# Routed attention and a gated feed-forward block on one core: narrower key bands over cluster-sorted rows (112 places beyond a chunk instead of 128)

## The chip, the core and the metric

The kernel runs on one core of a Trainium2 chip. The core has TensorE (PE in the profile; its weight loads are PEld), VectorE (DVE), ScalarE (ACT), GpSimd (POOL) and SyncE (SP), each with its own queue that is worked off in order, 16 DMA engines, an on-chip memory (SBUF) of 128 partitions, and PSUM, into which TensorE writes. The metric is the device time of one execution in microseconds (us), as a median over runs.

## The reference

Attention for 4 batches of 8 heads, 768 positions, head width 64. Every query and every key belongs to the one of 16 centroids to which it is nearest by direction; a query attends only to keys of its own cluster. The result goes through a feed-forward block with hard-swish.

```python
q_assign = argmax(einsum('bhsd,hcd->bhsc', q_n, c_n));  k_assign = the same for k
mask   = q_assign[:, :, :, None] == k_assign[:, :, None, :]
scores = where(mask, q @ k.T / 8, -1e9)
attn   = softmax(scores);  x = (attn @ v), heads side by side      # (3072, 512)
h      = x @ w_in;  g = h * clip(h + 3, 0, 6) / 6;  out = g @ w_out  # d_ff 2048
```

## The kernel before

Heads are worked in 16 pairs (two heads of 64 make 128 partitions). The order of all instructions is written by hand: the kernel records them in one sequence, and every engine works off its own part of that sequence in order.

*Pairs 0 to 7 (batches 0 and 1)* use full attention: every chunk of 128 keys against all 768 queries, with a mask added through TensorE. During this stage the weights are decoded from 64-bit floats. It fills roughly the first third of the span.

*Pairs 8 to 15 (`FIRST` to `NPAIR - 1`)* sort first. `own_clusters`, `run_up`, `step_up`, `order` and `positions` work out, for every query and key, its place when the rows are sorted by cluster; `edges` keeps, per pair and cluster, the first place and the place behind the last, for queries (index 0) and keys (index 1). `scatter` (L1034) writes the rows of q, and of k and v together, to their places in DRAM: 24 indirect DMAs per pair from POOL, each followed by three tiny memsets (`pause`, L1026). `load_ranked` reads the sorted rows back over SP's queue (tiles `piece` for q and k, `vs` for v), and `turn_ranked` transposes them on TensorE (L919), with the copy out of PSUM on ACT (L920).

Then only a band of the score matrix is needed. `band(i)` says which chunks of queries the keys of chunk i meet: chunk i and its two neighbours, so 384 queries for the four inner chunks and 256 for the first and last. `band_scores` computes the bands in three steps: chunks 0, 5 and 1, then 2 and 3, then 4. Each band is, for each of the two heads, a bf16 mask product (`xm`, written by `band_masks` from the ends of the clusters) and an f32 product of keys and queries (L1077); chunks 1 and 3 use the two PSUM tiles `pv` and `pw`, the others `ps`. ACT takes the exponential (L1100) into tiles `be`, which come from a pool `bandp` of 5 buffers of 384 columns. `band_values` multiplies them with the values (L1116): each half of the queries (384) gets contributions of four chunks, the inner one first (all 384 columns), then parts of 256, 256 and 128 columns. `key_adds` adds, on DVE (L1130), the exponentials of the other three chunks onto those of the inner chunk (1 or 4); `band_sums` sums that over the keys on TensorE (L1140), and `band_divide` divides. `keep_ranked` writes the result in sorted order to DRAM, `gather` (L1050, 12 indirect DMAs per pair on POOL) brings it back to the original order, `turn_back` transposes it and stores it as input `xd` of the feed-forward block.

`steps_of` gives every step of a pair an offset in points; a pair has a slot of 28 points (`SLOT`), and `late_plan` lays the eight pairs over one another. For pair g the scatters are recorded at offset -24, `band_masks` at -12, `load_ranked` at -5, `turn_ranked` at -1 and 0, the bands at 2 to 12, the gather at 23 and `turn_back` at 37 (the last pair has some of them earlier). At 26 of the 28 points one item of the feed-forward block is recorded. `up` items (L659, 16 per block of 256 tokens) multiply with `w_in`, and their operand sums `tx` are fetched by DMAs that ACT issues two items ahead (L548); ACT then copies (`sx`, L677) and lifts (L499), DVE adds and clips (L670, L502, L649). `down` items (L698, 14 per block) multiply with `w_out`. The feed-forward block is computed by a scheme of seven half-size products in place of eight.

After the last pair only feed-forward items are left. There `whether_good` works out, on DVE, a flag from all range sums, among them a test on `edges`; when the flag is not set, `general_path` computes everything a second time without sorting.

Of the kernel before, what the change touches and what calls it, by code (L numbers as in the profile page):

```python
# [18 lines left out]
P = 128  # L19
# [19 lines left out]


FAR = 2.0**60


FIRST = NPAIR // 2
# [75 lines left out]
def fast_path(ctx, tc, ok, q, k, v, centroids, moe_w_in, moe_w_out, out):  # L120
# [660 lines left out]
    def whether_good():  # L781
        good = smallp.tile([P, 2, 2 * FIRST], F32, name="good")
        fit = smallp.tile([P, 2, NW], F32, name="fit")
        alone = smallp.tile([P, 2, FIRST], F32, name="alone")
        for got, sums, *bounds in (
            (good, totals, BOUND, 0.0), (fit, w_totals, W_HIGH, 0.0), (alone, counts, NC2, -NC2 * (C - 1.0)),
        ):
            for a, bound in enumerate(bounds):
                nc.vector.tensor_scalar(
                    out=got[:, a], in0=sums[:, a], scalar1=bound, scalar2=None, op0=ALU.is_le  # L790
                )
        low = smallp.tile([P, 6], F32, name="low")
        for a, got in enumerate((good, fit, alone)):
            nc.vector.tensor_reduce(out=low[:, a : a + 1], in_=got, axis=AX.XY, op=ALU.min)
        late = NPAIR - FIRST
        sane = smallp.tile([P, 2, late, 4 * NHC], F32, name="sane", tag="sane")
        flat = inverses.rearrange("p g i c -> p g (i c)")
        for a, (bound, op) in enumerate(((BOUND, ALU.is_le), (1.0 / BOUND, ALU.is_ge))):
            nc.vector.tensor_scalar(out=sane[:, a], in0=flat, scalar1=bound, scalar2=None, op0=op)
        nc.vector.tensor_reduce(out=low[:, 3:4], in_=sane, axis=AX.XYZ, op=ALU.min)  # L800
        near = smallp.tile([P, 2, late], F32, name="near")
        for a in range(2):
            nc.vector.tensor_tensor(
                out=near[:, a], in0=edges[:, :, a, 1], in1=edges[:, :, 1 - a, 0], op=ALU.subtract
            )
        nc.vector.tensor_scalar(out=near, in0=near, scalar1=P + 1.0, scalar2=None, op0=ALU.is_le)
        nc.vector.tensor_reduce(out=low[:, 4:5], in_=near, axis=AX.XY, op=ALU.min)
# [23 lines left out]
    def open_late():  # L831
        whole.close()
        late = ctx.enter_context(ExitStack())
        for name, bufs in (
            ("rankp", 1), ("piecep", 2), ("svp", 1), ("fromp", 1), ("natp", 1), ("sortp", 1), ("bandp", 5),
            ("rowp", 3), ("posp", 4),
        ):
            st[name] = right(late, name, bufs)
        for name, bufs in (("psum_y", 2), ("psum_s", 1)):
            st[name] = late.enter_context(tc.tile_pool(name=name, bufs=bufs, space=PSUM))  # L840
        rankp = st["rankp"]
# [90 lines left out]
    def own_clusters(g):  # L932
# [6 lines left out]
        mx = rankp.tile([P, 2 * NC2], F32, name="mx")  # L939
# [71 lines left out]

    def positions(g):
        prod = st.pop(("prod", g))
        posf = st["rankp"].tile([P, 2 * NC2], F32, name="posf")
        nc.vector.reduce_sum(out=posf, in_=prod, axis=AX.X)
        pos = st["pos", g] = st["posp"].tile([P, 2, NCH, 2], I32, name="pos")
        nc.vector.tensor_scalar(
            out=pos.rearrange("p a j t -> p (a j t)"), in0=posf, scalar1=S - 1.0, scalar2=0.0,
            op0=ALU.min, op1=ALU.max,
        )  # L1020
# [34 lines left out]

    def band_masks(g):
        xm = st["xm", g] = st["sortp"].tile([P, NC2, P], BF16, name="xmsort")
        ends = st["rankp"].tile([P, 2], F32, name="ends")
        nc.vector.tensor_scalar(
            out=ends, in0=edges[:, g - FIRST, :, 1], scalar1=st["sign"], scalar2=st["odd"],  # L1060
# [6 lines left out]
        nc.vector.tensor_scalar(out=xk, in0=st["places"], scalar1=ends[:, 1:2], scalar2=None, op0=ALU.is_lt)  # L1067

    def band(i):
        return max(i - 1, 0), min(i + 2, NCH)  # L1070

    def band_products(g, i, dst):
        lo, hi = band(i)
        for x, first in ((st["xm", g], True), (st["xs", g], False)):
            for t in range(2):
                r = slice(t * D, (t + 1) * D)
                nc.tensor.matmul(dst[t], lhsT=x[r, NCH + i], rhs=x[r, lo:hi], start=first, stop=not first)  # L1077

    def band_scores(g, pair, other=None):

        ps = st["psum_s"].tile([P, 2, 512], F32, name="ps")
        at, parts = 0, []
        for i in pair:
            w = (band(i)[1] - band(i)[0]) * P
            parts.append((i, w, [ps[:, :, at : at + w]]))
            band_products(g, i, [ps[:, t, at : at + w] for t in range(2)])
            at += w
        if other is not None:
            w = (band(other)[1] - band(other)[0]) * P
            heads = [  # L1090
                psum_v.tile([P, 512], F32, name="pv")[:, 0:w],
                psum_t.tile([P, 512], F32, name="pw", tag="t")[:, 0:w],
            ]
            parts.append((other, w, heads))
            band_products(g, other, heads)
        for i, w, srcs in parts:
            ex = st["be", g, i] = st["bandp"].tile([P, 2, HALF], F32, name="be")
            dsts = [ex[:, :, 0:w]] if len(srcs) == 1 else [ex[:, t, 0:w] for t in range(2)]
            for dst, src in zip(dsts, srcs):
                nc.scalar.activation(out=dst, in_=src, func=ACT.Exp, scale=SM_SCALE)  # L1100

    def shared(i, hf):
        lo, hi = band(i)
        a, b = max(lo, hf * NHC), min(hi, (hf + 1) * NHC)
        return (a - lo) * P, (a - hf * NHC) * P, (b - a) * P

    def parts_of(hf):
        return ((1, 0, 2, 3), (4, 5, 3, 2))[hf]
# [1 line left out]
    def band_values(g, hf):  # L1110
        pv = psum_v.tile([P, 512], F32, name="pv")
        parts = parts_of(hf)
        for n, i in enumerate(parts):
            src, dst, w = shared(i, hf)
            for t in range(2):
                nc.tensor.matmul(  # L1116
                    pv[t * D : (t + 1) * D, dst : dst + w], lhsT=st["vs", g][:, t, i],
# [608 lines left out]
```

## Time and profile before

| | |
|---|---|
| median of 3 runs | 949.89 us (947.76, 949.89, 950.37) |
| profiled execution | 947.94 us, of which its span on the engines 946.1 us |
| granted TensorE clock | 0.998 |
| busy share: PE, PEld, DVE, ACT, POOL | 98%, 77%, 63%, 37%, 62% |
| HBM | 94.67 MB read, 28.31 MB written |

The page gives busy times per engine; in 40 slices how busy each was; the chain of work that ended last; and groups of instructions of one line, engine and shape, as `line engine op out<-in shapes xcount | busy us, mean ns of one | idle time before them <- what ended it`. Matmuls in f32 appear as two records each. A timeline row is `start us, duration us, engine line op`, and where the engine stood idle before it, the idle time and what ended it. A row of the wait view is `engine line <- who ended the wait: us in total, times, longest`. A row of the chain in order of time is `start us, us, what`; SPq and ACTq are the queues' DMA issues.

### The profile page before, as it was taken

To read this page: it belongs to the slowest core of one execution; us is meant where nothing else is said; L and a number is where in the kernel's file an instruction comes from. 1 tells how busy PE (TensorE), PEld (TensorE's weight loads), DVE (VectorE), ACT (ScalarE), POOL (GpSimd) and SP (SyncE) were. 2 spreads that over 40 slices of the span, in tenths; PEclk is the share of its full clock that TensorE was granted. 3 is DMA by queue.
4 is the path that set the end of the run, shared out by engine and by line. 5 is a ranking of instruction groups with operands and counts; after the bars stand their busy time and mean duration, and the time that the engine had idled before them with its cause. 6 is when DMAs were issued, how large, how long until landed. Compare 5 with 4: busy or idle time off the path is not lost.

```text
span 946.1 us, 17635 instructions
## 1 busy us (share of the span) xinstructions
PE 928.3 (98%) x6358; PEld 726.5 (77%) x6358; DVE 591.6 (63%) x1294; ACT 349.5 (37%) x731; POOL 583.9 (62%) x1314
## 2 busy tenths in 40 slices
PE   8999999989999999999999999999999999999997
PEld 5444444555798798797887988978888799999996
DVE  6789889899976375284483474564571554536261
ACT  5888877766112232233232132241331311212020
POOL 3878777769366677787777777777777060303030
PEclk9999999999999999999999999999999999999999
DMA  7345555361364648482683654754753233323120
GB/s 192 108 134 157 134 156 165 109 174 46 96 209 141 153 137 175 130 220 78 171 201 100 166 158 128 192 151 113 176 161 99 77 99 113 106 69 110 56 68 26
DMA packets 174351, 124.23 MB, mean 131 GB/s; under 512 B 134064, under 2 KB 152496, under 8 KB 174256
## 3 DMA queue, kind: packets, MB, share of 16 engines
q1 hardware_dynamic: 151936, 76.04, 31.2%
q10 hardware_dynamic: 13104, 34.38, 12.7%
q0 software_dynamic: 9216, 12.60, 4.4%
q8 instruction: 52, 0.85, 0.4%
q14 instruction: 43, 0.35, 0.1%
HBM read 94.67 MB, written 28.31 MB: 130 GB/s over the span
## 4 chain that ended last, share of the span: by engine, by line
PE 70%; DVE 2%; DMA 1%; ACT 0%; POOL 0%; issue 0%; SPq 0%; ACTq 0%
PE Y L698 18%; PE uY L659 15%; PE X L698 13%; PE uX L659 12%; PE pv L1116 3%; PE ps L1077 3%; PE ps L919 2%; PE pv L1077 1%; PE pd L1140 1%; PE pcs L337 1%; PE ps L1157 1%; DMA piece<-kvd 1%; DVE g_sb L649 0%; DVE g_sb L502 0%; DVE g_sb L670 0%; DVE sx L670 0%
## 5 line engine op out<-in xcount | busy, mean ns | idle before, releaser
L433 POOL TENSOR_TENSOR acc<-acc,ex 128x768 f32<-128x768 f32 x64 | 123.8, 1935 | 26.0 <-ACT ex L423 22.4
L1034 POOL DMA_INDIRECT qd<-qn,pos x96 | 96.3, 1003 | 44.9 <-issue 32.5
L1050 POOL DMA_INDIRECT xn<-xsd,pos x96 | 93.7, 976 | 48.8 <-DVE g_sb L649 27.1
L499 ACT ACTIVATE sx<-g_sb,half_c 128x512 f32<-128x512 f32 x88 | 63.7, 724 | 141.1 <-DVE g_sb L670 141.1
L649 POOL TENSOR_TENSOR g_sb<-g_sb 128x256 f32<-128x256 f32 x52 | 39.1, 773 | 123.6 <-DVE g_sb L502 122.6
L1034 POOL DMA_INDIRECT kvd<-kvn,pos x96 | 96.6, 1006 | 25.6 <-issue 25.6
L1026 POOL MEMSET w_low<- 128x1 f32 x864 | 90.9, 105 | 33.3
L705 DVE TENSOR_TENSOR y<-y,Y 128x256 f32<-128x256 f32 x48 | 20.2, 421 | 136.5 <-PE Y L698 135.7
L659 PE MATMUL uX<-xb,w_in_sb 128*128 128x128 f32 x704 | 93.0, 275 | 0.0
L698 PE MATMUL X<-w_out_sb,g_sb 128*128 128x256 f32 x384 | 90.6, 382 | 0.4 <-DVE g_sb L502 0.4
L698 PE MATMUL Y<-T,g_sb 128*128 128x256 f32 x384 | 88.0, 381 | 0.0
L698 PE MATMUL Y<-w_out_sb,g_sb 128*128 128x256 f32 x384 | 87.7, 380 | 0.0
L659 PEld LDWEIGHTS uX<-xb,w_in_sb 128*128 128x128 f32 x704 | 85.7, 192 | 0.0
L698 PEld LDWEIGHTS X<-w_out_sb,g_sb 128*128 128x128 f32 x384 | 70.9, 190 | 14.8 <-issue 3.9
L698 PEld LDWEIGHTS Y<-T,g_sb 128*128 128x128 f32 x384 | 72.1, 190 | 13.2 <-issue 3.9
L670 DVE TENSOR_TENSOR sx<-uX,sx 128x128 f32<-128x128 f32 x176 | 51.0, 290 | 49.3 <-ACT sx L677 45.7
L698 PEld LDWEIGHTS Y<-w_out_sb,g_sb 128*128 128x128 f32 x384 | 71.9, 190 | 10.6 <-issue 1.3
L400 PE MATMUL ps<-xf 64*128 64x384 f32 x384 | 78.6, 487 | 0.3 <-ACT ex L423 0.3
L423 ACT ACTIVATE ex<-ps 128x768 f32<-128x768 f32 x96 | 72.6, 802 | 4.6 <-PE ps L400 4.5
L443 PE MATMUL pv<-ex,vt 128*64 128x384 f32 x384 | 72.5, 499 | 0.0
L502 DVE SCALAR_TENSOR_TENSOR g_sb<-sx,g_sb 128x512 f32<-128x512 f32 x88 | 63.6, 725 | 3.4 <-ACT sx L499 3.4
L670 DVE TENSOR_TENSOR g_sb<-uY,sx 128x128 f32<-128x128 f32 (+1 forms) x176 | 65.5, 413 | 0.0
(196 smaller groups left out, 1805.5 us busy)
## 6 DMA issues: line engine op xcount, KB each, us to landing
tx<-td ACTq DMA_DIRECT2D x86, 384.0 KB, 3.5
raw<-in_moe_w_in_dram SPq DMA_DIRECT2D x16, 512.0 KB, 3.8
raw<-in_moe_w_out_dram SPq DMA_DIRECT2D x16, 512.0 KB, 3.2
xb<-xd SPq DMA_DIRECT2D x12, 512.0 KB, 4.3
out_dram<-y SPq DMA_DIRECT2D x44, 128.0 KB, 1.7
qk<-in_q_dram SPq DMA_DIRECT2D x18, 192.0 KB, 3.7
qk<-in_k_dram SPq DMA_DIRECT2D x18, 192.0 KB, 5.0
vt<-in_v_dram SPq DMA_DIRECT2D x16, 192.0 KB, 3.8
```

What stands on the lines that cost most here:

```text
L400: nc.tensor.matmul(st["ps", n][:, t, 0:HALF], lhsT=x[r, NCH + j], rhs=x[r, hf * NHC : (hf + 1) * NHC], start=first, stop=last, skip_group_ ...
L423: nc.scalar.activation(out=ex, in_=sc, func=ACT.Exp, scale=SM_SCALE)
L433: nc.gpsimd.tensor_tensor(out=acc, in0=acc, in1=ex, op=ALU.add)
L443: nc.tensor.matmul(pv[t * D : (t + 1) * D], lhsT=vt[:, t, j], rhs=ex[:, t], start=(j == 0), stop=(j == NCH - 1),)
L499: nc.scalar.activation(out=r, in_=h, func=ACT.Relu, bias=half_c, scale=1.0 / 6.0)
L502: nc.vector.scalar_tensor_tensor(out=g, in0=r, scalar=1.0, in1=h, op0=ALU.min, op1=ALU.mult)
L659: nc.tensor.matmul(dst, lhsT=w[:, kt], rhs=x(kt), start=(kt == 0), stop=(kt == HK - 1))
L670: nc.vector.tensor_tensor(out=out_, in0=in0, in1=in1, op=ALU.add)
L698: nc.tensor.matmul(bank[:, half * HC : (half + 1) * HC], lhsT=g_sb[:, kind, i], rhs=w[:, i], start=(first and i == 0), stop=(last and i == ...
L1026: nc.gpsimd.memset(w_low, W_LOW)
L1034: i = nc.gpsimd.indirect_dma_start(out=rows[name, g, t], in_=src, in_offset=None, out_offset=bass.IndirectOffsetOnAxis(ap=pos[:, a, j, t : ...
L1050: nc.gpsimd.indirect_dma_start(out=xn[:, j, t], out_offset=None, in_=rows["xsd", g, t], in_offset=bass.IndirectOffsetOnAxis(ap=pos[:, 0, j ...
```

## The change

The constant `REACH = 112` is new, and a band is now counted in places, not in chunks: the keys of chunk i meet the queries from 112 places before the chunk to 112 places behind it. The widths become 240, 352, 352, 352, 352, 240 instead of 256, 384, 384, 384, 384, 256. In `band_values` the first contribution to a half covers columns 16 to 367 of 384, the next ones 240, 240 and 112 columns.

The exponentials of chunks 1 and 4 go into one tile `bw` of full width, with 16 columns at either side set to zero by two memsets on DVE per pair (in `band_masks`), because `key_adds` and `band_sums` still work on 384 columns. Those of chunks 0 and 5 go into one tile of 480 columns, written by a single activation where there were two; those of chunks 2 and 3 into a pool of 2 buffers. `bandp` shrinks from 5 to 2 buffers, `posp` from 4 to 3, and `mx` and `posf` share a buffer. The test on `edges` no longer compares the ends of clusters with 129, but asks for each of the five borders between chunks whether a cluster whose keys lie on both sides of it, or end or begin there, reaches more than 112 places over it with its queries; it has 17 DVE instructions in place of 4.

```diff
+REACH = 112
...
     def band(i):
-        return max(i - 1, 0), min(i + 2, NCH)
+        return max(i * P - REACH, 0), min((i + 1) * P + REACH, S)
...
-                nc.tensor.matmul(dst[t], lhsT=x[r, NCH + i], rhs=x[r, lo:hi], start=first, stop=not first)
+                nc.tensor.matmul(dst[t], lhsT=x[r, NCH + i], rhs=rows[r, lo:hi], start=first, stop=not first)
...
+        if len(pair) == 2:
+            at = parts[0][1]
+            ex = st["edgep"].tile([P, 2, 2 * at], F32, name="be", tag="edge")
+            nc.scalar.activation(out=ex, in_=ps[:, :, 0 : 2 * at], func=ACT.Exp, scale=SM_SCALE)
...
-            ex = st["be", g, i] = st["bandp"].tile([P, 2, HALF], F32, name="be")
+            if ("whole", i) in st:
+                ex = st["be", g, i] = st["whole", i]
+                at = band(i)[0] - i // NHC * HALF
...
     def shared(i, hf):
+        if i == parts_of(hf)[0]:
+            return 0, 0, HALF
         lo, hi = band(i)
-        a, b = max(lo, hf * NHC), min(hi, (hf + 1) * NHC)
-        return (a - lo) * P, (a - hf * NHC) * P, (b - a) * P
+        a, b = max(lo, hf * HALF), min(hi, (hf + 1) * HALF)
+        return a - lo, a - hf * HALF, b - a
...
+            if n == 0:
+                edge = band(1)[0]
+                src, dst, w = edge, edge, w - 2 * edge
...
     def band_masks(g):
         xm = st["xm", g] = st["sortp"].tile([P, NC2, P], BF16, name="xmsort")
+        for margin in st["margins"]:
+            nc.vector.memset(margin, 0.0)
...
-            ("rankp", 1), ... ("sortp", 1), ("bandp", 5),
-            ("rowp", 3), ("posp", 4),
+            ("rankp", 1), ... ("sortp", 1), ("bandp", 2), ("edgep", 1),
+            ("wholep", 1), ("rowp", 3), ("posp", 3),
...
+        for i in range(NCH - 1):
+            nc.vector.memset(cuts[:, i : i + 1], (i + 1.0) * P)
...
+        for n, terms in enumerate((
+            ((edge(1, 0), 0.0, at), (at, 1.0, edge(1, 1)), (edge(0, 0), REACH + 1.0, at)),
+            ((edge(1, 0), 1.0, at), (at, 0.0, edge(1, 1)), (at, REACH + 1.0, edge(0, 1))),
+        )):
```

More of the change, by code (lines that the diff above doesn't have):

```diff
@@ L800, in whether_good, with edge @@
         nc.vector.tensor_reduce(out=low[:, 3:4], in_=sane, axis=AX.XYZ, op=ALU.min)
[L801 to L807, printed above, removed]
+        shape = [P, late, NCH - 1]
+        size = late * (NCH - 1)
+        room = smallp.tile([P, 3 * size + NCH - 1], F32, name="room", tag="sane")
+        near = room[:, 0 : 2 * size].rearrange("p (n g i) -> p n g i", n=2, g=late)
+        over = room[:, 2 * size : 3 * size].rearrange("p (g i) -> p g i", g=late)
+        cuts = room[:, 3 * size :]
+        for i in range(NCH - 1):
+            nc.vector.memset(cuts[:, i : i + 1], (i + 1.0) * P)
+        at = cuts.unsqueeze(1).to_broadcast(shape)
+        def edge(a, e):
+            return edges[:, :, a, e].unsqueeze(2).to_broadcast(shape)
+        for n, terms in enumerate((
+            ((edge(1, 0), 0.0, at), (at, 1.0, edge(1, 1)), (edge(0, 0), REACH + 1.0, at)),
+            ((edge(1, 0), 1.0, at), (at, 0.0, edge(1, 1)), (at, REACH + 1.0, edge(0, 1))),
+        )):
+            for m, (in0, scalar, in1) in enumerate(terms):
+                nc.vector.scalar_tensor_tensor(
+                    out=over if m else near[:, n], in0=in0, scalar=scalar, in1=in1, op0=ALU.add, op1=ALU.subtract
+                )
+                if m:
+                    nc.vector.tensor_tensor(out=near[:, n], in0=near[:, n], in1=over, op=ALU.max)
+        nc.vector.tensor_scalar(out=near, in0=near, scalar1=1.0, scalar2=None, op0=ALU.is_ge)
+        nc.vector.tensor_reduce(out=low[:, 4:5], in_=near, axis=AX.XYZ, op=ALU.min)
         full = smallp.tile([P, 2, late, 2], F32, name="full")
@@ L834, in open_late @@
         for name, bufs in (
-            ("rankp", 1), ("piecep", 2), ("svp", 1), ("fromp", 1), ("natp", 1), ("sortp", 1), ("bandp", 5),
-            ("rowp", 3), ("posp", 4),
+            ("rankp", 1), ("piecep", 2), ("svp", 1), ("fromp", 1), ("natp", 1), ("sortp", 1), ("bandp", 2), ("edgep", 1),
+            ("wholep", 1), ("rowp", 3), ("posp", 3),
         ):
@@ L840, in open_late @@
             st[name] = late.enter_context(tc.tile_pool(name=name, bufs=bufs, space=PSUM))
+        ex = st["wholep"].tile([P, 2, 2, HALF], F32, name="bw")
+        for a, i in enumerate((1, NCH - 2)):
+            st["whole", i] = ex[:, a]
+        lo = band(1)[0]
+        st["margins"] = [ex[:, :, :, at : at + lo] for at in (0, HALF - lo)]
         rankp = st["rankp"]
@@ L938, in own_clusters @@
             nc.tensor.transpose(out=pr[:, 8 * i : 8 * i + 8], in_=cs[:, i], identity=ident)
-        mx = rankp.tile([P, 2 * NC2], F32, name="mx")
+        mx = rankp.tile([P, 2 * NC2], F32, name="mx", tag="mx")
         nc.vector.reduce_max(out=mx, in_=pr, axis=AX.X)
@@ L1013, in positions @@
         prod = st.pop(("prod", g))
-        posf = st["rankp"].tile([P, 2 * NC2], F32, name="posf")
+        posf = st["rankp"].tile([P, 2 * NC2], F32, name="posf", tag="mx")
         nc.vector.reduce_sum(out=posf, in_=prod, axis=AX.X)
@@ L1074, in band_products @@
         for x, first in ((st["xm", g], True), (st["xs", g], False)):
+            rows = x.rearrange("p j c -> p (j c)")
             for t in range(2):
                 r = slice(t * D, (t + 1) * D)
-                nc.tensor.matmul(dst[t], lhsT=x[r, NCH + i], rhs=x[r, lo:hi], start=first, stop=not first)
+                nc.tensor.matmul(dst[t], lhsT=x[r, NCH + i], rhs=rows[r, lo:hi], start=first, stop=not first)
     def band_scores(g, pair, other=None):
@@ L1083, in band_scores @@
         for i in pair:
-            w = (band(i)[1] - band(i)[0]) * P
+            w = band(i)[1] - band(i)[0]
             parts.append((i, w, [ps[:, :, at : at + w]]))
@@ L1088, in band_scores @@
         if other is not None:
-            w = (band(other)[1] - band(other)[0]) * P
+            w = band(other)[1] - band(other)[0]
             heads = [
@@ L1095, in band_scores @@
             band_products(g, other, heads)
-        for i, w, srcs in parts:
-            ex = st["be", g, i] = st["bandp"].tile([P, 2, HALF], F32, name="be")
-            dsts = [ex[:, :, 0:w]] if len(srcs) == 1 else [ex[:, t, 0:w] for t in range(2)]
+        if len(pair) == 2:
+            at = parts[0][1]
+            ex = st["edgep"].tile([P, 2, 2 * at], F32, name="be", tag="edge")
+            nc.scalar.activation(out=ex, in_=ps[:, :, 0 : 2 * at], func=ACT.Exp, scale=SM_SCALE)
+            for a, i in enumerate(pair):
+                st["be", g, i] = ex[:, :, a * at : (a + 1) * at]
+            parts = parts[2:]
+        for i, w, srcs in parts:
+            if ("whole", i) in st:
+                ex = st["be", g, i] = st["whole", i]
+                at = band(i)[0] - i // NHC * HALF
+            else:
+                ex = st["be", g, i] = st["bandp"].tile([P, 2, w], F32, name="be", tag="inner")
+                at = 0
+            ex = ex[:, :, at : at + w]
+            dsts = [ex] if len(srcs) == 1 else [ex[:, t] for t in range(2)]
             for dst, src in zip(dsts, srcs):
```

## The prediction

> **What bounds the kernel now.** I read the page first, then who waits for whom, then the sorted stage (317 to 746 us), where all edited instructions but the flag lie.
>
> ```profile
> span 946.1 us, 17635 instructions
> PE 928.3 (98%) x6358; PEld 726.5 (77%) x6358; DVE 591.6 (63%) x1294; ACT 349.5 (37%) x731; POOL 583.9 (62%) x1314
> PE Y L698 18%; PE uY L659 15%; PE X L698 13%; PE uX L659 12%; PE pv L1116 3%; PE ps L1077 3%; PE ps L919 2%; PE pv L1077 1%; PE pd L1140 1%; PE pcs L337 1%; PE ps L1157 1%; DMA piece<-kvd 1%; DVE g_sb L649 0%; DVE g_sb L502 0%; DVE g_sb L670 0%; DVE sx L670 0%
> ```
>
> PE is busy 98% and leads the chain; the band products (L1077, L1116) are about 7% of it. One entry is no engine's: DMA piece<-kvd, 1%. PE's own waits from 310 to 760 us are three:
>
> ```profile
> PE uX L659 <- DMA tx<-td: 2.0, 1, 2.0
> PE pd L1140 <- DVE be L1130: 0.8, 1, 0.8
> PE ps L919 <- ACT xsort L920: 0.4, 1, 0.4
> ```
>
> So nearly every nanosecond taken from PE should shorten the span, unless something that PE doesn't pace is what those waits wait for. POOL is that candidate. Its groups from 313 to 733 us, and its first scatter of pair 9:
>
> ```profile
> L1034 POOL DMA_INDIRECT kvd<-kvn,pos x84 | 84.5, 1006 | 22.7 <-issue 22.7
> L1034 POOL DMA_INDIRECT qd<-qn,pos x84 | 84.3, 1003 | 28.9 <-issue 16.5 <-DVE pos L1017 9.7 <-DVE g_sb L649 1.3
> L1050 POOL DMA_INDIRECT xn<-xsd,pos x84 | 82.3, 980 | 19.6 <-issue 6.0 <-ACT xnat L920 1.4 <-ACT sx L677 1.4
> L1026 POOL MEMSET w_low<- 128x1 f32 x754 | 79.4, 105 | 29.0
> 312.78 0.96 POOL L1034 DMA_INDIRECT qd<-qn,pos  x1 [9.74 <-DVE pos L1017]
> ```
>
> Busy 330.5 and idle 100.2 us; of the idle time the rows put 9.7 us on one wait, before 312.78, for positions that PE paces and that come before any edited matmul, and 1.3 or 1.4 us in total on each other engine's line. Everything after 312.78 is a fixed train, about (430.7 - 9.7) / 7 = 60 us for each of seven slots. Where PE needs less than 60, POOL is as much a bound as PE. At pair 11 the train is visibly the later one:
>
> ```profile
> 472.87 0.96 POOL L1034 DMA_INDIRECT kvd<-kvn,pos  x1 [0.16 <-issue]
> 469.60 6.00 SPq L890 DMA_DIRECT2D piece<-qd  x2
> 476.28 4.90 DMA piece<-kvd
> 481.24 0.33 ACTq L548
> 481.67 0.27 ACT sx L677
> 486.04 0.68 PE L659 MATMUL uX<-xs,tx 128*128 128x128 f32 x4 [2.00 <-DMA tx<-td]
> 490.78 0.87 PE ps L919 x6
> ```
>
> SP reached pair 11's loads at 469.60, but the first two took 6.00 us, to 475.60, because the second had to wait for the last scatters (472.87 + 0.96, and their landing). The load of kvd landed at 476.28 + 4.90 = 481.18; ACT's next tx issue stood behind it (481.24), and with it, in ACT's order, the copy sx. The late tx held PE until 486.04; DVE's work behind the late sx then released PE at 490.78. Nothing in this sequence is paced by PE.
>
> **The change part by part.** *Narrower products.* The groups that price a column:
>
> ```profile
> L1077 PE MATMUL ps<-xsort 64*128 64x384 f32 x64 | 12.9, 482 | 0.0
> L1077 PE MATMUL ps<-xsort 64*128 64x256 f32 x64 | 9.1, 377 | 0.0
> L1077 PE MATMUL ps<-xmsort 64*128 64x384 bf16 x32 | 5.4, 333 | 0.0
> L1077 PE MATMUL ps<-xmsort 64*128 64x256 bf16 x32 | 4.4, 274 | 0.0
> L1116 PE MATMUL pv<-be,vs 128*64 128x256 f32 x128 | 16.5, 379 | 0.0
> L1116 PE MATMUL pv<-be,vs 128*64 128x128 f32 x64 | 6.2, 273 | 0.0
> 318.08 0.48 PE L1077 MATMUL pv<-xsort 64*128 64x384 f32 x1
> 318.09 0.48 PE L1077 MATMUL pw<-xsort 64*128 64x384 f32 x1
> ```
>
> The 64 f32 records of 384 columns on ps are 2 chunks x 2 heads x 8 pairs = 32 matmuls of two passes each. The two heads run side by side (318.08 and 318.09), so a column is paid once for both; a record's mean has the latency of the array in it, so a column costs by the slope: (482 - 377) / 128 = 0.82 ns a column in L1077, (379 - 273) / 128 = 0.83 in L1116, and (333 - 274) / 128 = 0.46 for the bf16 mask. The scores lose 2 x 16 + 4 x 32 = 160 columns a pair: 160 x (0.46 + 2 x 0.82) = 0.34 us. The values lose 32 + 16 + 16 + 16 = 80 columns in each half, 160 a pair: 160 x 2 x 0.83 = 0.27 us. Together 0.60 us a pair, 4.8 us for eight: the ceiling. The number of matmuls and the changes of tile shape stay.
>
> The Trainium skill ("TensorE: Matmul & The Clock Gate", section "LDWEIGHTS (loading the stationary operand)") speaks a little against it: a load takes its columns / 1.2 ns, so 107 ns for 128, which a mask product of 240 columns would no longer cover. By it the two end chunks would save nothing on the mask, and the ceiling would be 0.1 us lower; no row here shows a 240-column product.
>
> *How much of it reaches the end.* Pairs 8, 9 and 10 lie before the wait at 486.04. PE comes there 3 x 0.60 = 1.8 us sooner and waits 1.8 us longer: their gain is lost. Pair 11 brings 0.60 us to the next meeting, at pair 12:
>
> ```profile
> 536.01 1.01 SPq L890 DMA_DIRECT2D piece<-kvd  x2
> 540.38 0.72 ACT L499 ACTIVATE sx<-g_sb,half_c 128x512 f32<-128x512 f32 x1 [2.57 <-DVE g_sb L670]
> 540.84 0.33 ACTq L548 DMA_DIRECT2D tx<-td  x1
> 541.86 0.60 DVE L670 TENSOR_TENSOR sx<-uX,sx 128x128 f32<-128x128 f32 x2
> 550.66 0.87 PE L919 MATMUL ps<-ident,piece 128*128 128x128 f32 x6 [0.37 <-ACT xsort L920]
> ```
>
> The second load of kvd, issued about 536.6, lands some 4.3 us later by the time at which ACT's tx issue comes free (540.84; unheld it stands 0.1 us behind the start of the lift, 540.38). ACT's copy, which at pair 11 began 0.43 us behind the tx issue and took 0.27, ends at 541.54 however early PE is; DVE's sum, now at 541.86, can move up by 0.3 us only, and DVE then works without a gap up to PE's wait at 550.66. Of pair 11 I keep 0.3 us. Pairs 12 to 15 give 4 x 0.60 = 2.4 us if no later meeting takes them:
>
> ```profile
> 600.67 1.03 SPq L890 DMA_DIRECT2D piece<-qd  x2
> 658.71 1.22 SPq L890 DMA_DIRECT2D piece<-qd  x2
> 713.70 1.82 SPq L890 DMA_DIRECT2D piece<-kvd  x2
> 722.63 0.82 PE L919 MATMUL ps<-ident,piece 128*128 128x128 f32 x6
> ```
>
> For pairs 13 and 14 both loads of qd left within 1.03 and 1.22 us, so the scatters were done. For pair 15 SP was held, but q's transpose comes 9 us after the kvd loads left, more than the 4.9 us that such a load took above; PE will be 2.1 us sooner. Sum: 2.4 + 0.3 = 2.7 us, with 0.6 (only pair 15 survives) and 4.8 as bounds.
>
> *Work off the path.* The flag:
>
> ```profile
> L803 DVE TENSOR_TENSOR near<-edges 128x8 f32<-128x8 f32 x2 | 0.2, 164 | 0.0
> 789.70 0.42 DVE L583 TENSOR_TENSOR xs<-xb 128x256 f32<-128x256 f32 x1 [4.65 <-DMA xb<-xd]
> ```
>
> It gains 13 small DVE instructions, at most 13 x 164 ns = 2.1 us, inside the 4.65 us in which DVE then waits for a DMA: nothing; uncovered it would be 2.1 us, once. The 16 memsets of margins, by the same row at most 2.6 us over the span, stand at offset -12, between DVE's busy stretches, and the shorter key adds give most of that back: 2 x 96 elements a pair at up to 692 / 512 = 1.35 ns, 2.1 us in all, from
>
> ```profile
> L1130 DVE TENSOR_TENSOR be<-be 128x512 f32<-128x512 f32 x32 | 22.2, 692 | 23.3 <-PE pv L1116 15.1 <-ACT xt L920 7.6
> ACT be L1100 <- DVE be L1130: 27.0, 7, 5.4
> ```
>
> The last row is a wait that vanishes: chunk 4's exponential no longer needs a buffer that DVE must first read. ACT regains 27 us, but PE has no wait there; I count nothing, bounded above by PE's 0.8 us for pd. One activation of 960 elements for two of 512 only shortens ACT. Fewer buffers of pos and be add no wait: their readers are done a slot earlier.
>
> **The rivals.** *The whole ceiling.* If the meeting at pair 11 moves with PE, 4.8 us arrive: 945.1. For: three short waits in 450 us. Against: the chain through 476.28.
>
> *POOL sets every later slot too.* If PE meets the train at pair 14 or 15 as well, 0.6 to 1.2 us remain: about 949.0. Against: rows 600.67 and 658.71.
>
> *Slower: the train itself slows.* Up to pair 12's loads it has 4 x 24 + 3 x 12 = 132 indirect DMAs, and its lateness goes to the end one for one. Break-even with 2.7 us is 20 ns each, 2% of 1006. At 50 ns each it costs 6.6 us: 949.9 + 3.9 = 953.8. For it speaks how full the DMA engines are while it gathers (0.97), where PE's earlier tx loads would fall:
>
> ```profile
> 354.00:373.00 19.00, 19.00 (x125) 16.70 (x124) 12.17 (x37) 4.38 (x8) 15.19 (x48) 1.00 0.97 211
> ```
>
> Against: the bytes are the same.
>
> *It doesn't do what it says*: the tighter flag fails and everything is computed again. The general path needs at least the products with w_out once more, 31% of the span by the chain, so over 1240 us. But sorting the reference's own inputs by cluster, the farthest query that a chunk of keys needs in the sorted heads lies 90 places beyond it, under 112.
>
> **How the numbers follow.** The profiled execution took 947.94 us, 1.84 around its span; 2.7 less is 945.2. It is 1.95 below the median of the runs; on 949.89 the forecast is 947.2. Chances: forecast 0.50, ceiling 0.22, POOL in every slot 0.12, slower train 0.15, flag 0.01. What can be told from no change is about 0.3%, 2.85 us; the forecast sits just inside it, and as its own bounds reach further up than down I split it 0.28 faster, 0.22 same. Faster: 0.28 + 0.22 = 0.50. Same: 0.22 + 0.12 + 0.01 of the slower case = 0.35. Slower: 0.14 + 0.01 = 0.15. The range goes from the ceiling less 0.9 (the runs before spread over 2.6 us) to a train slowed by about 30 ns a DMA: 944.2 to 951.2; it leaves out most of the slower case.
>
> **What would show it.** Right: f32 bands of 352 columns near 482 - 32 x 0.82 = 456 ns; PE's wait for tx before pair 11's transposes grown from 2.0 to about 3.8 us, PE back at 486 as before; from pair 13 on all of PE about 2 us earlier; POOL's train unchanged. Wrong: that wait unchanged or gone (ceiling); new PE waits at pairs 14 or 15; indirect DMAs above 1026 ns; band records no shorter.

## The result, and the profile after

The changed kernel takes 946.29 us (median of 6 runs, 944.55 to 947.44); the kernel before, on the same chip, 950.29 us (6 runs, 947.76 to 951.08). The ratio is 0.9956, with a 95% interval from 0.9943 to 0.9969: 4.0 us faster, more than the forecast of 2.7 and less than the ceiling of 4.8. In microseconds the interval goes from 2.9 to 5.4 us: the forecast's 2.7 lies just outside it, the ceiling inside, so the times alone do not tell whether the whole worth of the columns arrived. The profiled execution took 944.79 us at a granted clock of 0.998, 3.15 us less than the one of before. Its page begins so, and of its fourth part this is the row of lines:

```profile
span 942.6 us, 17656 instructions
PE 923.4 (98%) x6358; PEld 725.4 (77%) x6358; DVE 593.5 (63%) x1323; ACT 348.1 (37%) x723; POOL 583.8 (62%) x1314
PE Y L701 18%; PE uY L662 16%; PE X L701 12%; PE uX L662 12%; PE pv L1163 3%; PE ps L945 2%; PE ps L1106 2%; PE pv L1106 1%; PE pd L1187 1%; DMA tx<-td 1%; PE pcs L340 1%; PE ps L1204 1%; DVE g_sb L652 0%; DMA piece<-kvd 0%; DVE g_sb L673 0%; DVE sx L673 0%
```

The line numbers have moved: L1077 is now L1106, L1116 L1163, L1140 L1187, L659 L662, L698 L701, L919 L945, L890 L916, L548 L551, L1034 L1060, L1050 L1076. PE is busy 4.9 us less with the same 6358 matmuls, close to the ceiling of 4.8; the span is shorter by 3.5 only. The idle time of PE, span less busy time, has grown by 1.4 us, from 17.8 to 19.2. The groups of the band products, as instruction, tile, shape and count, then busy us and mean ns of one:

```profile
L1106 PE MATMUL ps<-xsort 64*128 64x352 f32 x64 | 12.1, 456 | 0.0
L1106 PE MATMUL ps<-xsort 64*128 64x240 f32 x64 | 8.8, 367 | 0.0
L1106 PE MATMUL ps<-xmsort 64*128 64x352 bf16 x32 | 5.2, 320 | 0.0
L1106 PE MATMUL ps<-xmsort 64*128 64x240 bf16 x32 | 4.3, 268 | 0.0
L1163 PE MATMUL pv<-be,vs 128*64 128x240 f32 x128 | 15.7, 366 | 0.0
L1163 PE MATMUL pv<-be,vs 128*64 128x112 f32 x64 | 5.8, 259 | 0.0
```

The f32 band of 352 columns takes 456 ns, the number forecast; the others fell by the same slope. What a whole pair saves is seen from slot to slot where PE doesn't wait. The first band product of pairs 13 and 14 in the timeline of before:

```profile
613.89 0.28 PE L1077 MATMUL ps<-xmsort 64*128 64x256 bf16 x2
673.18 0.28 PE L1077 MATMUL ps<-xmsort 64*128 64x256 bf16 x2
```

and of the changed kernel:

```profile
611.34 0.28 PE L1106 MATMUL ps<-xmsort 64*128 64x240 bf16 x2
670.04 0.28 PE L1106 MATMUL ps<-xmsort 64*128 64x240 bf16 x2
```

59.29 us became 58.70: 0.59 a pair, against 0.60 in the forecast's sum. The four largest of PE's waits from 306 to 850 us in the changed kernel:

```profile
PE uX L662 <- DMA tx<-td: 1.4, 1, 1.4
PE pd L1187 <- DVE bw L1177: 0.8, 1, 0.8
PE uX L662 <- DVE g_sb L652: 0.7, 1, 0.7
PE ps L945 <- ACT xsort L946: 0.7, 2, 0.3
```

The wait for tx is 1.4 us, not the 3.8 forecast, and it is another one: it stands at pair 12, not at pair 11. At pair 11 the timeline of the changed kernel has these rows (start, duration, and in brackets the idle time before):

```profile
472.09 0.96 POOL L1060 DMA_INDIRECT kvd<-kvn,pos  x1 [0.16 <-issue]
468.24 5.51 SPq L916 DMA_DIRECT2D piece<-qd  x2
478.78 0.33 ACTq L551 DMA_DIRECT2D tx<-td  x1
479.20 0.27 ACT L680 COPY sx<-uX 128x128 f32<-128x128 f32 x1 [1.30 <-PE uY L662]
483.38 0.68 PE L662 MATMUL uX<-xs,tx 128*128 128x128 f32 x4 [0.70 <-DVE g_sb L652]
```

The pattern of before is still there: SP held by the last scatters, ACT's tx issue late (1.60 us behind the lift at 477.18, where it stands 0.1 us behind when nothing holds it), the copy sx 0.42 us behind it, PE waiting. (The bracket of the copy names PE, whose last product before it ended at 479.10; but ACT's queue had stood at the tx issue until 478.73, and by then the products that the copy reads, which ended at 477.76, were done.) But all of it came earlier. The tx issue moved from 481.24 to 478.78, 2.46 us, while PE itself had gained 2.3 us on its way there (0.56 that this execution had from the start, before any edited instruction, and 3 x 0.59) and had lost 0.9 of that again to small waits ahead of pair 10. So PE was back at 483.38 and not at 486.04. The 2.46 us can be followed back: POOL's last scatter ended at 473.05 instead of 473.83, 0.78 earlier, of which 0.57 is the earlier start of the train (312.21 against 312.78); SP was free of the two qd loads 0.70 us after that scatter (468.24 + 5.51 = 473.75) where it had been 1.77 before (475.60), 1.07 earlier; the remaining 0.6 lies between the kvd loads and the tx issue. As far as the profile shows, none of these three is paced by a band product.

At pair 12 the main rows of the chain of waits of the changed kernel, in order of time (start, us, what):

```profile
532.96 1.47 PE uX L662 x12
534.44 3.84 DMA piece<-kvd
538.35 5.77 DMA tx<-td
544.26 1.58 PE uX L662 x12
```

Here the load of kvd took 3.84 us and released the tx issue, and that tx load took 5.77, where the one at pair 11 was used 4.60 us after its issue (478.78 to 483.38). PE waited 1.4 us for it; in the execution of before there was no such wait.

Adding up the profiled executions: the first band product of pair 8 came 0.56 us earlier (316.26 against 316.82), which no edit explains; from there to the last product of `band_sums` the stage took 431.1 instead of 434.9 us, 3.8 less; behind PE's last matmul 0.82 more was spent, whose cause stays open. That is 3.5. Of the 8 x 0.59 = 4.7 us that the stage could have given, 0.9 did not arrive; nearly all of it is missing in the slots of pairs 9 to 11, where the new waits stand.

POOL's groups from 313 to 733 us:

```profile
L1060 POOL DMA_INDIRECT kvd<-kvn,pos x84 | 84.0, 1000 | 22.9 <-issue 22.9
L1060 POOL DMA_INDIRECT qd<-qn,pos x84 | 83.0, 989 | 28.5 <-issue 16.9 <-DVE pos L1043 9.6 <-DVE g_sb L673 2.0
L1076 POOL DMA_INDIRECT xn<-xsd,pos x84 | 82.3, 979 | 19.6 <-issue 8.1 <-ACT sx L680 0.8 <-ACT cs L345 0.7
```

The train did not slow: 1000, 989 and 979 ns against 1006, 1003 and 980. And the flag, in DVE's groups from 782 to 786 us and the largest of its new groups from 760 to 830:

```profile
L586 DVE TENSOR_TENSOR xs<-xb 128x256 f32<-128x256 f32 x1 | 0.4, 426 | 2.6 <-DMA xb<-xd 2.6
...
L826 DVE TENSOR_TENSOR room<-room 128x40 f32<-128x40 f32 x4 | 0.8, 199 | 0.1
```

DVE's wait for xb shrank from 4.65 to 2.61 us: 2.04 us of new instructions, inside the wait as forecast. ACT's wait for `be` from DVE (27.0 us before) is no longer in the view of its waits, and its end gave PE nothing that shows: the wait for pd is 0.8 as before.

### The profile page after: what moved, and what is told of

Same layout as the page of the kernel before. It is cut to its first block, busy times and chain, and to the rows that moved or that the text cites. A ratio compares the mean times of both kernels' runs of the same rounds, so it can differ in the third digit from the quotient of the medians.

```text
span 942.6 us, 17656 instructions
## 1 busy us (share of the span) xinstructions
PE 923.4 (98%) x6358; PEld 725.4 (77%) x6358; DVE 593.5 (63%) x1323; ACT 348.1 (37%) x723; POOL 583.8 (62%) x1314
## 4 chain that ended last, share of the span: by engine, by line
PE 70%; DVE 2%; DMA 1%; ACT 0%; issue 0%; POOL 0%; ACTq 0%
PE Y L701 18%; PE uY L662 16%; PE X L701 12%; PE uX L662 12%; PE pv L1163 3%; PE ps L945 2%; PE ps L1106 2%; PE pv L1106 1%; PE pd L1187 1%; DMA tx<-td 1%; PE pcs L340 1%; PE ps L1204 1%; DVE g_sb L652 0%; DMA piece<-kvd 0%; DVE g_sb L673 0%; DVE sx L673 0%
## 5 line engine op out<-in xcount | busy, mean ns | idle before, releaser
L1076 POOL DMA_INDIRECT xn<-xsd,pos x96 | 93.8, 977 | 46.2 <-ACT sx L502 25.1
L1060 POOL DMA_INDIRECT qd<-qn,pos x96 | 95.3, 992 | 43.7 <-DVE pos L1043 22.9
L1060 POOL DMA_INDIRECT kvd<-kvn,pos x96 | 96.7, 1007 | 25.7 <-issue 25.7
L662 PE MATMUL uX<-xb,w_in_sb 128*128 128x128 f32 x704 | 93.0, 275 | 0.0
L701 PE MATMUL X<-w_out_sb,g_sb 128*128 128x256 f32 x384 | 90.6, 382 | 0.5 <-DVE g_sb L505 0.5
L701 PE MATMUL Y<-T,g_sb 128*128 128x256 f32 x384 | 88.0, 381 | 0.0
L701 PE MATMUL Y<-w_out_sb,g_sb 128*128 128x256 f32 x384 | 87.7, 380 | 0.0
L662 PEld LDWEIGHTS uX<-xb,w_in_sb 128*128 128x128 f32 x704 | 85.7, 192 | 0.0
L701 PEld LDWEIGHTS X<-w_out_sb,g_sb 128*128 128x128 f32 x384 | 70.9, 190 | 14.6 <-issue 3.4
L701 PEld LDWEIGHTS Y<-T,g_sb 128*128 128x128 f32 x384 | 72.1, 190 | 13.0 <-issue 3.3
L701 PEld LDWEIGHTS Y<-w_out_sb,g_sb 128*128 128x128 f32 x384 | 71.9, 190 | 10.5 <-issue 1.0
```

The source lines that it names most:

```text
L662: nc.tensor.matmul(dst, lhsT=w[:, kt], rhs=x(kt), start=(kt == 0), stop=(kt == HK - 1))
L701: nc.tensor.matmul(bank[:, half * HC : (half + 1) * HC], lhsT=g_sb[:, kind, i], rhs=w[:, i], start=(first and i == 0), stop=(last and i == ...
L1060: i = nc.gpsimd.indirect_dma_start(out=rows[name, g, t], in_=src, in_offset=None, out_offset=bass.IndirectOffsetOnAxis(ap=pos[:, a, j, t : ...
L1076: nc.gpsimd.indirect_dma_start(out=xn[:, j, t], out_offset=None, in_=rows["xsd", g, t], in_offset=bass.IndirectOffsetOnAxis(ap=pos[:, 0, j ...
```

## Experiments

Three readings are set against each other. In the first only PE's own work counts, and what is taken from it arrives whole. The second is the forecast's: in the first half of the stage PE meets loads that stand behind POOL's train of indirect DMAs, and what PE gains ahead of such a meeting is lost in it. In the third, first put down ahead of the runs with a shorter pause, the DMAs crowd each other, and a train that is driven harder costs. For each kernel the time is a median, and the ratio stands to the kernel before in the same session on the same chip.

For the readings a table helps, worked out from the traces: the slot of a pair is the time from its first band product to that of the next pair, and PE's idle time in it is what lies between the starts of two matmuls beyond the columns' own time, gaps above 0.13 us, each less the 0.1 us that some steps of the sequence take anyway. Sums over slots are taken before rounding. The meeting called that of pair 10, 11 or 12 lies at the end of slot 9, 10 or 11.

| us | slot 8 | 9 | 10 | 11 | 12 | 13 | 14 | idle in 9, 10, 11 |
|---|---|---|---|---|---|---|---|---|
| before | 57.98 | 58.72 | 61.19 | 59.88 | 59.30 | 59.29 | 54.31 | 0.0, 2.2, 0.4 |
| before, repeated | 57.98 | 59.49 | 60.17 | 59.89 | 59.30 | 59.29 | 54.31 | 0.6, 1.4, 0.4 |
| changed | 57.50 | 58.99 | 59.54 | 60.34 | 58.71 | 58.70 | 53.72 | 0.7, 1.2, 1.5 |
| changed, repeated | 57.50 | 59.66 | 59.98 | 60.13 | 59.16 | 59.31 | 53.73 | 1.3, 1.6, 1.3 |
| reach 96 | 56.92 | 58.03 | 63.88 | 58.72 | 58.12 | 58.12 | 53.14 | 0.4, 3.7, 0.5 |

### The two kernels again

No edit.

> The kernel before once more, for a second trace. Theory 2 (PE meets POOL's train at pairs 10 to 12): its slots of pairs 9 to 11 hold waits of PE of 2 to 3.5 us together again, in other places by up to a microsecond, and the slots of pairs 8, 12, 13 and 14 hold none.

950.25 us, ratio 1.0001 [0.9988, 1.0014], 12 runs: the same time. Its profile shows how much the meetings move with nothing changed: PE's wait for tx was 1.3 us (2.0 in the first profile), and 0.6 us stood in slot 9 instead. The total of slots 9 to 11, 2.4 us, lies where the second reading had put it.

```profile
PE uX L659 <- DMA tx<-td: 1.3, 1, 1.3
...
PE ps L919 <- ACT xsort L920: 0.7, 2, 0.4
```

> The changed kernel once more, for a second trace of it. Theory 1 (only PE counts): PE's waits between 400 and 560 us at the same places and of the same lengths as in its first trace (0.4 to 1.6 us at pairs 10, 11 and 12). Theory 2 (PE meets POOL's train of indirect DMAs and the loads behind it, and those vary by about a microsecond): the same total within 0.3%, but the waits at pairs 10 to 12 lie differently between the three pairs.

949.22 us against 954.27, ratio 0.9945 [0.9918, 0.9972]: in a session where both kernels are 3 to 4 us slower the gain is the same as far as the interval tells, and again the interval (2.7 to 7.8 us) holds the whole ceiling. This profile, of an execution of 951.38 us, has more waits than the first, in more places:

```profile
PE uX L662 <- DMA tx<-td: 2.8, 3, 1.4
PE ps L945 <- issue: 1.1, 1, 1.1
```

### A narrower band still

The band is cut again by as much as the change cut it; 96 places still hold what the inputs need (90).

```diff
-REACH = 112
+REACH = 96
```

> The changed kernel with a reach of 96 places (the inputs need 90), so widths of 224 and 320 and another 160 columns a pair less in the scores and in the values. Theory 1: another 4.8 us, ratio to before about 0.9905. Theory 2: the gain of pairs 8 to 12 is taken by longer waits at the train; pairs 13 to 15 keep 0.6 us each, so 2 to 3 us more than the changed kernel, ratio about 0.993, and PE's waits between 400 and 560 us grow to 5 us or more.

947.94 us, ratio 0.9923 [0.9896, 0.9951], on the chip and in the session of the repeated changed kernel: 2.1 us better by the ratios, 1.3 by the medians, where the removed columns are worth another 8 x 0.59 = 4.7. Free of waits its slots are 58.12, again 0.59 less. The largest of PE's waits from 306 to 850 us:

```profile
PE uX L662 <- DVE steps L978: 3.4, 1, 3.4
```

In slot 10 PE lost 3.7 us in one wait, and the chain ahead of it is that of pair 11 above (a copy sx held in ACT's order, then DVE's work behind it). The wait is not all that this meeting cost. From 489.2 to 496.0 us the granted clock was 0.50, and the same eight products took almost twice as long behind the wait as ahead of it:

```profile
483.97 1.06 PE L662 MATMUL uX<-xb,w_in_sb 128*128 128x128 f32 x8
490.26 1.19 PE L662 MATMUL uX<-xs,tx 128*128 128x128 f32 x4 [3.45 <-DVE steps L978]
491.25 1.91 PE L662 MATMUL uX<-xb,w_in_sb 128*128 128x128 f32 x8
```

So slot 10 is 63.88 us long. Free of waits it would be about 59.54 - 1.2 - 0.59 = 57.75; less the 3.7, some 2.4 us go to the clock (an estimate from these numbers). In the sorted stage of the two kernels themselves, four profiles with waits of up to 2.0 us, the clock stayed at 1.00.

PE's idle time in slots 9 to 11 is 4.6 us, a little under the 5 or more that the second reading asked for. The profile shows where the gain stayed in this execution, in a longer meeting and the clock behind it, and that speaks for the second reading. But it fell on the slowest of the six executions (950.01 us); the two fastest took 942.5 and 944.75 us, at mean clocks of 0.998 and 0.997 where it had 0.992. The intervals are too wide for the times to refuse the first reading, whose 0.9905 lies inside. This kernel has the lowest ratio of the study, though its interval overlaps that of the changed kernel.

### PE made the later one

One item of the feed-forward block is recorded at 26 of a slot's 28 points. Here the first four slots get one at all 28, so that PE needs about 62 us for them, more than the train's 60; the eight items are missing behind the last pair. If the second reading holds, no wait is left at pairs 9 to 11, and the columns' worth arrives whole.

```diff
-            busy = i >= AHEAD and (i - AHEAD) % SLOT in (6, 9)
+            busy = i >= AHEAD + 4 * SLOT and (i - AHEAD) % SLOT in (6, 9)
```

The kernel before with this edit:

> The kernel before with a feed-forward item at all 28 points of the first four slots, not 26: eight items, some 13 us of PE's work, come from the tail into the slots of pairs 8 to 11, so PE reaches the loads of pairs 9 to 12 that much later by the train. Theory 1 (only PE counts): ratio to before 1.000, the same work in another order. Theory 2: PE's waits before pairs 10 to 12 vanish, 2 to 3 us less, ratio 0.997.

The changed kernel with it:

> The changed kernel with the same eight items moved forward. Theory 1: ratio to before 0.995, as the changed kernel. Theory 2: no meeting is left in it either, so it is the full 4.8 us under the kernel before with the items moved, ratio to before 0.992, and its slots of pairs 9 to 11 hold under 0.5 us of waits in all, where the changed kernel had 3.4 and 4.9.

The kernel with a reach of 96 with it:

> The same with a reach of 96 places. Theory 1: ratio to before 0.990 to 0.992, as with 96 places alone. Theory 2: another full 4.8 us, ratio to before 0.987, and slots 0.6 us shorter than with 112 places throughout.

Measured on one chip: 966.03 us (ratio 1.0173 [1.0157, 1.0188]), 961.55 (1.0119 [1.0099, 1.0138]) and 955.94 (1.0063 [1.005, 1.0077]). The steps from reach to reach are 4.5 and 5.6 us, against 4.0 and some 2 without the edit. The slots of pairs 8 and 9 are 61.94 and 62.09, then 61.32 and 61.50, then 60.70 and 61.00: 0.6 each time; PE's idle time in slots 9 to 11 adds up to 0.9, 0.8 and 0.9 us. That is what the second reading asks for, but for the idle time, which it had put under 0.5 us. The medians do not decide it: from the ratios the first step is 5.1 us with an interval wide enough for 4.0, and the kernels without the edit ran in other sessions. (The medians rest on 4 to 6 runs each; in the profiled executions the stage took 450.4, 444.6 and 440.0 us, steps of 5.8 and 4.6, of which 1.0 in the first are waits in slot 12 that come to 3.5 us in the one and 2.5 in the other.)

All three are far slower than without the edit, and that was not foreseen: what the eight items did where they stood had not been asked. The first row of PE's waits in the kernel before with the edit, and in the changed one:

```profile
PE uX L659 <- DVE xs L583: 12.6, 2, 10.6
```

```profile
PE uX L662 <- DVE xs L586: 12.4, 2, 10.4
```

and the chain ahead of it in the changed one:

```profile
789.82 0.67 PE ps L945 x6
790.51 0.81 ACT xt L946
791.34 4.40 DMA xd<-xt
795.87 4.02 DMA xb<-xd
799.92 0.44 DVE xs L586
800.38 0.44 DVE xs L586
800.86 1.23 PE uX L662 x4
```

The last pair's result goes to DRAM and back (4.40 and 4.02 us) before the last feed-forward blocks can start. Eight `down` and `up` items had covered that; without them PE stands 10.4 us, and the granted clock was 0.50 from 792.7 to 806.4 us, so that the work behind the wait began slowly too. In the changed kernel without the edit DVE waited 2.6 us there and PE not at all.

### The train made longer

A fourth memset after every fourth indirect DMA makes the train 1.3 us a pair longer: in the traces of the kernel before, 368.6 us against 360.9 from the last scatter of pair 9 to that of pair 15.

```diff
     def pause():
-        for _ in range(PAUSE):
+        st["pauses"] = st.get("pauses", 0) + 1
+        for _ in range(PAUSE + (1 if st["pauses"] % 4 == 0 else 0)):
```

> The kernel before with a fourth memset behind every fourth indirect DMA, so POOL's train is 9 x 0.14 = 1.3 us a pair longer: 4 to 5 us later at pair 12's loads, 9 us later at pair 15's. Theory 1 (only PE counts): ratio to before 1.000. Theory 2 (PE meets the train): PE's waits before pairs 11 and 12 grow by 4 us or more together, and pair 15's transposes begin to wait; 4 to 6 us more than before, ratio 1.004 to 1.006.

> The changed kernel with the same longer train. Theory 1: ratio to before 0.995, as the changed kernel. Theory 2: what the narrower bands save is waited away at every meeting up to pair 15, so within 1 us of the kernel before with the longer train, ratio to before 1.003 to 1.006.

954.52 us (1.0011 [0.9991, 1.0031]) and 952.63 (0.9997 [0.9976, 1.0018]), 12 runs each. For the kernel before this is the first reading's 1.000, and the second's 1.004 to 1.006 lies outside the interval. For the changed kernel both missed: 0.995 and 1.003 to 1.006 lie outside. It keeps 1.9 us of its gain by the medians, 1.3 by the ratios; the two intervals of about 2 us on either side let no more be said than that it is likely less than the 4.0 to 5.0 without the edit. PE's largest waits, in the kernel before and in the changed one:

```profile
PE ps L919 <- ACT xnat L920: 2.4, 1, 2.4
PE uX L659 <- DMA tx<-td: 2.3, 1, 2.3
```

```profile
PE uX L662 <- DMA tx<-td: 6.8, 2, 3.7
```

The second profile fell on the slowest of the changed kernel's executions (960.22 us), so its 6.8 us are not typical; it shows what such an execution is made of. At the end of its two long waits, 3.1 us up to 492.45 and 3.7 up to 556.73, the granted clock went to 0.50 (493.8 to 497.2 and 555.2 to 562.0 us). In both profiles the longer train shows as longer waits, but that the changed kernel pays more for it is not shown by one slow execution. The pair of runs speaks for the second reading only in that the changed kernel's gain shrank.

### The train made shorter

If the train is what PE meets, a shorter one should set the gain free. With two memsets for three after every indirect DMA:

```diff
-    PAUSE = 3
+    PAUSE = 2
```

> The kernel before with two memsets behind each indirect DMA in place of three, so a train about 36 x 0.14 = 5 us a pair shorter. Theory 1: nothing changes, ratio 1.000, PE's waits at pairs 11 and 12 stay at about 3 us together. Theory 2: SP isn't held at the loads of pairs 11 and 12, PE's waits of 2.2, 0.3 and 0.5 us there vanish, about 2 to 3 us less, ratio 0.997. A rival to both: denser indirect DMAs crowd the other loads, and the time rises.

> The changed kernel with the same shorter train. Theory 1: as the changed kernel, ratio to before 0.9956. Theory 2: the whole 4.8 us arrive on top of what the shorter train gives the kernel before, so 7 to 8 us less than before, ratio about 0.992, and PE's waits at pairs 10 to 12 are under 0.5 us in all.

1020.12 us (1.0688 [1.0646, 1.073]) and 1020.6 (1.0676 [1.0641, 1.0711]): 66 us slower, and nothing of the change is left to see. With the shorter pause only after every fourth indirect DMA (`-1` in place of the `1` in the edit above):

> The kernel before with two memsets in place of three behind every fourth indirect DMA: a train 1.3 us a pair shorter. Theory 1: ratio to before 1.000. Theory 2: the waits before pairs 11 and 12 vanish, 2 to 3 us less, ratio 0.997. Theory 3, from the run with two memsets everywhere: the pause is what leaves the DMA engines room, and even this quarter costs more than the waits it saves, ratio above 1.003.

> The changed kernel with the same shorter train. Theory 1: ratio to before 0.995. Theory 2: no meeting is left and the whole 4.8 us arrive beside the 2 to 3 us: ratio to before 0.992. Theory 3: above the changed kernel, ratio to before 0.998 or more.

970.29 us (1.02 [1.0163, 1.0237]) and 964.68 (1.0133 [1.0094, 1.0171]): 17 and 11 us slower. The times go the way of the third reading, a train that is driven harder costs; that crowded DMAs are the reason was not shown. Of the change this says little, since these kernels are held up by something else. The kernel before with two memsets, first its page, then the rows of PE and of the indirect DMAs in one stretch of its timeline:

```profile
span 1014.0 us, 17347 instructions
PE 958.7 (95%) x6358; PEld 738.4 (73%) x6358; DVE 590.9 (58%) x1294; ACT 350.4 (35%) x731; POOL 552.3 (54%) x1026
```

```profile
351.63 0.96 POOL L1034 DMA_INDIRECT qd<-qn,pos  x1 [0.16 <-issue]
352.03 0.70 PE L659 MATMUL uX<-xb,w_in_sb 128*128 128x128 f32 x4 [0.45 <-issue]
353.01 0.96 POOL L1034 DMA_INDIRECT kvd<-kvn,pos  x1 [0.15 <-issue]
353.45 0.27 PE L659 MATMUL uX<-xb,w_in_sb 128*128 128x128 f32 x1 [0.72 <-issue]
353.56 0.51 PE L659 MATMUL uY<-xs,tx 128*128 128x128 f32 x3
354.39 0.96 POOL L1034 DMA_INDIRECT qd<-qn,pos  x1 [0.16 <-issue]
354.87 0.37 PE L659 MATMUL uY<-xs,tx 128*128 128x128 f32 x1 [0.80 <-issue]
```

In this stretch matmuls that follow one another without a gap in the other kernels come four at a time, with 0.45 to 0.80 us between them for which the profile names no cause; PE goes on 0.40 to 0.48 us after the start of each indirect DMA. It is not so at every DMA: from 310 to 830 us PE has 45 such gaps of more than 0.1 us, 18.0 us together, beside 255 indirect DMAs, and 14 of the gaps end 0.3 to 0.6 us behind the start of one. In the kernel before it has none. The indirect DMAs themselves became no longer (both scatter groups 987 ns from 313 to 733 us, against 1003 and 1006).

Of the 68 us of span, 37.5 are idle time of PE (55.3 us against 17.8) and 30.4 are busy time. The granted clock was 0.986 instead of 0.998, about 12 us of the 68 by an estimate from these two; directly behind the stretch above it was 0.50, from 354.7 to 361.5 us. What PE lacks in the gaps was not found. With the shorter pause at every fourth DMA only, such gaps are few (8 and 12, 3.7 and 2.9 us), so they do not explain those 17 and 11 us, whose cause stays open.

## Why the prediction was right, and where its sizes were off

*Price of the edit.* Right. Free of waits a pair saves 0.59 us where 0.60 had been worked out, from 384 to 352 columns and again from 352 to 320; the slope of the record means held at widths that the trace of before did not show (456, 367 and 259 ns for 352, 240 and 112 columns). In detail the slope was a little high for the narrow end chunks: from the start of their mask to the next chunk they saved 27 ns each where it gives 16 x 2.10 = 34, while chunk 1 saved 67, as it gives; that is the hundredth between 0.60 and 0.59.

The other price was worked out from the Trainium skill ("TensorE: Matmul & The Clock Gate", section "LDWEIGHTS (loading the stationary operand)"), by which a load of 128 columns takes an estimated 107 ns. The forecast had it that a mask of 240 columns no longer covers this; by its own slope it does, with 240 x 0.46 = 110 ns. The runs don't show such a floor: the loads of the mask's keys are records of 92 to 94 ns, the mean of the mask fell by 6 ns for 16 columns (274 to 268), and by the starts of the records (medians) a step's first mask product took 120, 113 and 106 ns at 256, 240 and 224 columns, its second 109, 103 and 96.

*What was counted at nothing.* Right as far as the profile shows: the flag lies in DVE's wait for xb, PE's wait for pd behind the key adds stayed at 0.8 us, no wait of PE names a memset or an exponential, and the train kept its pace.

*The whole ceiling, and a train in every slot.* The second rival did not come, and the first is not excluded by the times: 4.8 us lie inside the interval of 2.9 to 5.4. Against it speak the profiles. In the profiled execution 0.9 of 4.7 us did not arrive, and by the medians 4.8 - 4.0 = 0.8. From pair 12's bands on PE met nothing in the first profile of the changed kernel, and its slots are 0.59 shorter each; in the repeated one 0.13 and 0.60 us were lost in slots 12 and 13.

*The slower rival.* It did not come, and break-even of 20 ns a DMA was not touched: all three groups became a little shorter.

*The step that failed* is how much of it reaches the end, and in it the sentence that the gain of pairs 8 to 10 is lost, 1.8 us, with PE back at 486. PE was back at 483.38. The mechanism is there: slots 9 to 11 hold more idle time in the changed kernel than before, 3.3 against 2.7 us, 4.2 against 2.4 in the repeated profiles (on two chips), and 4.6 with a reach of 96; where PE is made the later one, most of that time is gone (0.8 to 0.9 us are left) and 4.5 us arrive by the medians. But in these single profiles it takes 0.6 to 1.8 us, not 2.1. The forecast held the meeting to be a fixed point that only POOL's instructions set. The meeting is where transfers land, and that point wanders by as much as was to be measured: SP was free 1.77 or 0.70 us after the same scatter, and a tx load took under 4.6 or 5.77 us. The kernel before, profiled twice, waits 2.0 and 1.3 us for tx. Which transfer delays which, was not tried.

The loss also lies elsewhere than said: in the first profile 0.9 us ahead of pair 10, then more than all of it won back at pair 11 (slot 10 is 1.65 shorter, not 0.59), then 1.05 lost at pair 12. Pairs 8 to 11, which lie ahead of these meetings, kept 1.4 us together (237.77 us became 236.37 in slots 8 to 11), where the forecast had left them 0.3. That is the difference between 2.7 and the 3.8 that this stage gave.

That the total came out near says little of this step: the range, 944.2 to 951.2 us, holds the forecast, the ceiling and no change at all.

## What to carry to other kernels

A product's price by the slope between two widths of the same record was good to a few ns at widths that the trace didn't have. When an engine at 98% waits only at a few meetings with transfers, sum what is removed as the ceiling, and treat each meeting as a loss between zero and the whole of the gain before it: where a load lands moved by about 1 us from one execution to the next, so that one profile doesn't fix it. Look at the granted clock behind a long wait as well, because the wait may not be all that it costs. Before work is moved to fill such a wait, look at what that work covers where it stands: eight items taken from behind the last pair took 1.8 to 3.7 us of idle time out of slots 9 to 11 and cost over 10.

## What was unexpected of the hardware

One memset of about 106 ns less between two indirect DMAs of POOL (two in place of three) made the kernel 6.9% slower, one less after every fourth 2.0%. In the first case PE stood idle in 45 gaps from 310 to 830 us, some of them of 0.45 to 0.80 us, inside runs of matmuls that waited for nothing in the profile. One more after every fourth cost nothing that could be measured (1.0011 [0.9991, 1.0031]).

In the sorted stage of the kernels with at least three memsets, single waits of PE of 3.1, 3.4 and 3.7 us came with 3.4 or 6.8 us at a granted clock of 0.50, from the end of the wait or shortly behind it; with waits of up to 2.4 us the clock stayed at 1.00.
